# The last chunks routed one by one, and smaller bursts of loads: a DeltaNet block with a routed mixture of experts on one core

## The chip, the cores and the metric

The kernel runs on one core of a Trainium2 chip. The metric is the device time of one execution in microseconds (us). Engines: TensorE multiplies matrices (PE in the profile, PEld for its loads of weights), VectorE (DVE), ScalarE (ACT) and GpSimd (POOL) work elementwise, SyncE (SP) issues most transfers.

## The reference

The first half is DeltaNet attention: 4 batches of 8 heads, 768 tokens of width 48, one state of 48x48 for each batch and head, updated token by token. The second half reads its output as 3072 rows of width 384 and sends each row to one of 16 experts (the best of 4 groups, and in it the best of 4 experts), weighted by both softmaxes.

```python
for t in range(S):
    y[:, :, t] = einsum('bhd,bhde->bhe', q[:, :, t], state)
    v_old = einsum('bhde,bhd->bhe', state, k_n[:, :, t])
    state = state + b_t * einsum('bhd,bhe->bhde', k_n[:, :, t], v[:, :, t] - v_old)
...
ye = maximum(x[rows_of_e] @ w1[g, e], 0) @ w2[g, e]
out[rows_of_e] = g_w * e_w * ye
```

## The kernel before

**Attention.** The 768 tokens are cut into 24 chunks of 32; with 4 batches a chunk has 128 rows, one for each partition. Inside a chunk the token-by-token updates are a triangular system: `gram` (L248) multiplies a chunk's keys and queries with its keys, `inverse(g)` (on VectorE, for four chunks at once) inverts the triangles, and `spread` scales the inverse into the blocks `mtb` that PE takes as weights. `advance(u)` is the recurrence of chunk u. On PE it issues, in this order, a_ps (L486, the state times the keys), o_ps (L495, the state times the queries), w_ps (L503, the inverse times what is left of the values), s_ps (L514, the update of the state, kept in PSUM), and the second part of o_ps (L528). ScalarE copies the results out: f, w, s_bd (the state in SBUF, L520), x (the chunk's output rows). The next chunk's a_ps needs s_bd, so this is a chain from chunk to chunk. Between these matmuls stand a transposition of x (t_ps, L554) and the 20 scores of the gate (l_ps, L451 and L456), and the gram of the chunk ten places ahead (`LEAD`).

**Prologue.** Grams 0 to 9 run ahead of chunk 0. SP loads keys and queries (`load_kq`), the values and keys in another layout (`load_kv`, `kv` in the rows) and constants (`load_con`). All loads after the first go in bursts: `begin` (L797) writes one column of the target from ScalarE, and SP's load waits for that write. The table `bursts` says behind which gram a burst starts; `after_gram` does the same for grams 8 and 9. Two matmuls with 384 columns of constants (L834, 4 in the trace, where each 4-byte matmul is two) stand ahead of chunk 0. Gram 10 is issued in chunk 0, between w_ps and s_ps.

**Routing.** `route(r)` sends a group of chunks, given by `cuts`, to the experts: on VectorE the best score, the one-hot `hots` of the expert and the running count `acc`, on PE the rank of each row in its expert (L451, `s_ps<-hots,con` and `s_ps<-acc,con`), then on VectorE and ScalarE weights, place, the matrices `mine` (what to store) and `at` (where). The sort on PE (L722, `mine` and `at`) adds them into one bank, which holds for each expert's slots the token's row and its weight. The groups are chunks 0-5, 6-11, 12-17, 18-19, 20-21 and 22-23. Sorts of the first chunks are done as they come; in chunk 22 all that are left of chunks 0 to 19 are done, `read_found` (L868) copies the bank to `found`, and `gather_first` starts two indirect gathers of the rows of expert 0 that are known by then from the output x in DRAM. The rows that chunks 20 to 23 add to expert 0 come by matmuls with `at` (`add_near`), and the gathered rows by matmuls with the identity (`add_gathered`, both L852), all into three banks x_ps, which ScalarE copies to `xt_first`.

**Experts.** `order_experts` ranks the experts by their counts; expert 0 is fixed as the first (`FIXED`), the others come in the order of their counts, each with a fixed number of slots. For each expert PE multiplies 48 h_ps matmuls (L1112) and 48 y_ps (L1131); rows come by indirect gathers on POOL and are transposed on PE (t_ps, L1076) for expert 1 first.

**What sets the order.** The whole first half stands under a manual schedule: each engine runs its instructions in the order in which the program issues them. Tasks (`inverse`, `route`) are generators; `work(n)` gives each task a budget in proportion to n and its rate and pushes the ones that have some, and a task that yields a word (`ACT_STEP`, `SORT`, `READY`) is held until `allow` of that word. The main loop for chunk u (L887 to L995) and a tail behind it (L996 to L1030) call them by hand.

## Time and profile before

| | |
|---|---|
| runs of the kernel before | 491.49, 494.62 and 495.47 us, median 494.62 |
| the profiled execution | 493.09 us |
| its span | 491.1 us, mean granted clock of PE 0.976 |
| PE busy | 450.0 us (92% of the span) |
| DVE, ACT, POOL busy | 240.6, 192.8, 176.8 us |
| chunk 1's first a_ps | starts at 46.70 us |
| chunk 23's first a_ps | starts at 206.70 us |
| expert 0's first h_ps | starts at 220.38 us |

A row of the timeline gives the start in us, the busy time, the engine, the line of the kernel, the operation, the tile written and the tiles read, the shape and how many instructions are put together (each matmul of 4-byte data counts twice). In square brackets is the engine's idle time before it and what ended it; "issue" means that nothing which the profile shows ended it. A row of the stretches gives its bounds, its length, the busy time of PE, PEld, DVE, ACT and POOL, the granted clock of PE as a share of full speed, the share of the DMA engines and the rate.

### The profile page before, as it was taken

Reading aid. Unit: us, or ns where it says so; the run is one execution under the profiler, and the core shown is the slowest. Engines: PE = TensorE matmul, PEld = TensorE weight load, DVE = VectorE, ACT = ScalarE, POOL = GpSimd, SP = SyncE. Lnnn points to the kernel's source line nnn. Section 1 sums busy time; section 2 is a strip of 40 time slices with the busy share of each in tenths; the row PEclk is TensorE's granted clock in tenths of the full one; section 3 lists DMA queues with packets and bytes.
Section 4 is the critical chain, followed back from the end, with each engine's and each line's share of the span. In section 5 each row is a group of like instructions: output and inputs, shape, how many; then the busy total and the mean of one; then the engine's idle time right before and its main releaser. Section 6 shows DMA issues by size and latency. Waiting matters only on the chain.

```text
span 491.1 us, 18102 instructions
## 1 busy us (share of the span) xinstructions
PE 450.0 (92%) x7730; PEld 425.9 (87%) x7730; DVE 240.6 (49%) x872; ACT 192.8 (39%) x413; POOL 176.8 (36%) x300
## 2 busy tenths in 40 slices
PE   3338999999999999999999999999999999999992
PEld 3335888888888888789999999999999999999992
DVE  4988998997999998565201201220122112201110
ACT  3335579688897976541112111111211111111120
POOL 0031310415416400103456355544745456255131
PEclk9999599899999999999999999999999999999997
DMA  5566344455434455307977877858997789778820
GB/s 163 149 186 200 100 150 153 128 151 174 144 109 123 145 161 166 90 23 177 370 238 229 277 254 208 300 186 274 318 298 228 255 302 322 248 215 273 308 80 27
DMA packets 56757, 97.07 MB, mean 198 GB/s; under 512 B 18974, under 2 KB 41433, under 8 KB 56675
## 3 DMA queue, kind: packets, MB, share of 16 engines
q1 hardware_dynamic: 50755, 85.89, 54.6%
q0 software_dynamic: 5920, 10.00, 6.5%
q8 instruction: 62, 1.02, 0.9%
q14 instruction: 20, 0.16, 0.1%
HBM read 81.75 MB, written 14.27 MB: 196 GB/s over the span
## 4 chain that ended last, share of the span: by engine, by line
PE 55%; DMA 12%; issue 11%; ACT 7%; DVE 7%; POOL 7%; SPq 0%; POOLq 0%; DVEq 0%
PE y_ps L1131 16%; PE h_ps L1112 16%; DMA out_dram<-yo,to_i 7%; POOL xq L1084 5%; DMA kqt<-in_kq_dram 4%; PE w_ps L503 4%; PE s_ps L514 3%; ACT s_bd L520 3%; PE a_ps L486 2%; PE o_ps L528 2%; PE o_ps L495 2%; DVE m L388 2%; DVE below L382 2%; PE t_ps L554 2%; PE l_ps L456 1%
## 5 line engine op out<-in xcount | busy, mean ns | idle before, releaser
L1131 PE MATMUL y_ps<-hid,w 128*128 128x224 f32 (+15 forms) x768 | 132.2, 332 | 0.0
L1131 PEld LDWEIGHTS y_ps<-hid,w 128*128 128x128 f32 x768 | 129.1, 190 | 0.3
L1112 PE MATMUL h_ps<-xt,w 128*128 128x232 f32 (+14 forms) x720 | 122.7, 330 | 0.0
L1112 PEld LDWEIGHTS h_ps<-xt,w 128*128 128x128 f32 x720 | 120.1, 190 | 0.3
L1084 POOL DMA_INDIRECT xq<-x_dram,from_q x92 | 87.6, 952 | 35.0 <-issue 24.1
L1134 DVE COPY yt<-y_ps 128x232 f32<-128x232 f32 (+13 forms) x14 | 5.1, 365 | 144.4 <-PE y_ps L1131 144.4
L1115 ACT ACTIVATE hid<-h_ps 128x448 f32<-128x448 f32 (+15 forms) x64 | 32.1, 501 | 100.2 <-PE h_ps L1112 98.2
L1143 POOL DMA_INDIRECT out_dram<-yo,to_i x32 | 34.1, 1065 | 93.2 <-DVE yo L1181 83.7
L1136 ACT ACTIVATE yt<-y_ps 128x224 f32<-128x224 f32 (+15 forms) x34 | 11.4, 336 | 116.6 <-PE y_ps L1131 116.6
L382 DVE TENSOR_TENSOR below<-m 128x16 f32<-128x16 f32 (+4 forms) x180 | 53.3, 299 | 0.2
L388 DVE TENSOR_TENSOR m<-m,below 128x16 f32<-128x16 f32 (+4 forms) x180 | 53.0, 295 | 0.4
L520 ACT ACTIVATE s_bd<-s_ps 48x768 f32<-48x768 f32 x46 | 37.0, 804 | 5.6 <-PE s_ps L514 5.1
L1181 DVE TENSOR_SCALAR yo<-yr,gate 128x384 f32<-128x384 f32 (+14 forms) x28 | 11.1, 420 | 39.8 <-DMA yr<-y_dram 31.4
L503 PEld LDWEIGHTS w_ps<-f,mtb 64*64 64x64 f32 x736 | 24.6, 141 | 6.0 <-ACT f L490 3.9
L503 PE MATMUL w_ps<-f,mtb 64*64 64x48 f32 x736 | 27.5, 227 | 1.4 <-ACT f L490 1.4
L427 ACT ACTIVATE mtb<-mt,con 128x256 f32<-128x256 f32 x39 | 28.0, 741 | 0.0
L514 PE MATMUL s_ps<-w,kv 32*112 32x96 f32 x736 | 25.3, 273 | 0.9 <-ACT found L871 0.3
L514 PEld LDWEIGHTS s_ps<-w,kv 32*112 32x112 f32 x736 | 21.3, 178 | 3.8 <-ACT w L507 1.5
L528 PE MATMUL o_ps<-w,gqm 64*64 64x48 f32 x576 | 21.4, 225 | 2.5 <-issue 2.3
L486 PE MATMUL a_ps<-s_bd,kqt 112*32 112x96 f32 x736 | 21.1, 257 | 1.1 <-ACT s_bd L520 1.1
L495 PE MATMUL o_ps<-s_bd,kqt 112*32 112x96 f32 x736 | 21.8, 259 | 0.2 <-issue 0.2
L528 PEld LDWEIGHTS o_ps<-w,gqm 64*64 64x64 f32 x576 | 19.1, 139 | 3.3 <-issue 2.5
(184 smaller groups left out, 543.8 us busy)
## 6 DMA issues: line engine op xcount, KB each, us to landing
w<-in_w_dram SPq DMA_DIRECT2D x29, 1536.0 KB, 10.7
kv<-in_kv_dram SPq DMA_DIRECT2D x24, 416.0 KB, 3.2
kqt<-in_kq_dram SPq DMA_DIRECT2D x20, 448.0 KB, 4.8
x_dram<-x SPq DMA_DIRECT2D x24, 192.0 KB, 2.2
w<-in_w_dram SPq DMA_DIRECT2D x24, 128.0 KB, 3.8
y_dram<-yq SPq DMA_DIRECT2D x36, 84.0 KB, 9.4
yr<-y_dram SPq DMA_DIRECT2D x14, 192.0 KB, 2.5
kqt<-in_kq_dram SPq DMA_DIRECT2D x8, 224.0 KB, 3.6
```

Of the source, the lines that this page charges most:

```text
L382: nc.vector.tensor_tensor(t, column.to_broadcast(like), row.to_broadcast(like), op=ALU.mult)
L388: nc.vector.tensor_tensor(to, to, t, op=ALU.add)
L495: nc.tensor.matmul(o_ps[quads[b], 2 * j:2 * j + 2, :], lhsT=kqt[0:KR, 1, j, quads[b]], rhs=s_bd[0:KR, b, j], start=(j == 0), stop=False, s ...
L503: nc.tensor.matmul(w_ps[b, h], lhsT=mt[b, uu * H + (h % 2) * NP + h // 2], rhs=f[b, h], start=(h == 0), stop=True, skip_group_check=True)
L514: nc.tensor.matmul(s_at[0:KR, b, j], lhsT=k[quads[b], j, 0:KR], rhs=w[quads[b], 2 * j:2 * j + 2], start=(u == 0 and j == 0), stop=True, sk ...
L520: nc.scalar.activation(s_bd[rows, :, :, hh, :], s_at[rows, :, :, hh * D:(hh + 1) * D], ACT.Copy)
L528: nc.tensor.matmul(o_ps[b, h], lhsT=gq[b, hq].rearrange("p a t -> p (a t)"), rhs=w[b, h], start=(u == 0 and h == 0), stop=True, skip_group ...
L1084: nc.gpsimd.indirect_dma_start(out=xq[:, g, :], out_offset=None, in_=x_dram[:, :].rearrange("n (q c) -> (n q) c", q=4), in_offset=bass.Ind ...
L1112: nc.tensor.matmul(h_ps[:, k], lhsT=w1[:, j, (f + k) * 128:(f + k + 1) * 128], rhs=xt[:, j, 0:R], start=(j == 0), stop=(j == DC - 1), skip ...
L1115: nc.scalar.activation(hid[:, f:f + 2], h_ps, ACT.Relu)
L1131: nc.tensor.matmul(y_ps, lhsT=w2[:, f, j * 128:(j + 1) * 128], rhs=hid[:, f], start=(f == 0), stop=(f == FC - 1))
L1143: put = nc.gpsimd.indirect_dma_start(out=out[:, :], out_offset=bass.IndirectOffsetOnAxis(ap=to[0:P, i:i + 1], axis=0), in_=yo[0:P, :], in_ ...
```

## The change

Five things, by the program's own names.

1. **Groups.** `cuts` becomes 0, 6, 12, 18, 20, 21, so chunk 20 is a group of its own, and its rows are sorted ahead of the read of `found`; three chunks (21, 22, 23) instead of four are left for `add_near`. Each of them is routed by a new task, `route_near(u)`, alone. It has its exponential on ScalarE ahead of the ranks, the sums of the weights on POOL, and ranks in a bank of PSUM of its own.
2. **Gathered rows.** `turn_gathered` transposes the gathered rows of expert 0 in six steps into a bank that the scores use otherwise, and one ScalarE copy takes them out as `turned_rows`. VectorE then adds them to the three banks x_ps (`first_in`), where ScalarE copied before.
3. **Order of experts.** `order_experts` runs as a whole behind the addition of `found`, where a first part ran ahead of it.
4. **Prologue.** The bursts are smaller and begin behind earlier grams; chunks 10 and 11 are loaded ahead of chunks 8 and 9, which come last, and chunk 12 is loaded at the end of chunk 0. Gram 10 runs in the prologue, behind gram 9.
5. **spread.** The first block of chunks 16 to 19 is scaled on VectorE instead of ScalarE.

```diff
-            1: [of_kq(RG), of_kq(RG + 1)],
-            RG: [of_kq(RG + 2), of_kq(RG + 3)],
-            RG + 2: [of_kq(u, 1) for u in range(RG)]
-                    + [(wr[:, 0], [lambda: nc.sync.dma_start(out=wr, in_=wr_d)])],
-            2 * RG: [(kv_[0], [lambda: load_kv(0), lambda: load_con(1), lambda: load_kv(1)])],
-            2 * RG + 2: [of_kq(2 * RG), of_kq(2 * RG + 1)],
+            1: [of_kq(u) for u in range(RG, 2 * RG - 1)],
+            RG: [of_kq(2 * RG - 1), of_kq(0, 1), of_kq(1, 1)],
+            RG + 1: [of_kq(2, 1), of_kq(3, 1),
+                     (wr[:, 0], [lambda: nc.sync.dma_start(out=wr, in_=wr_d)])],
+            RG + 2: [(kv_[0], [lambda: load_kv(0), lambda: load_con(1)])],
+            RG + 3: [(kv_[1], [lambda: load_kv(1)]), of_kq(2 * RG + 2)],
+            2 * RG: [(kv_[2], [lambda: load_kv(2)])],
+            2 * RG + 1: [of_kq(2 * RG + 3)],
+            2 * RG + 2: [of_kq(2 * RG)],
+            2 * RG + 3: [of_kq(2 * RG + 1)],
         }
-        after_gram = {2 * RG: [of_kq(2 * RG + 2), (kv_[2], [lambda: load_kv(2)])],
-                      2 * RG + 1: [of_kq(2 * RG + 3), of_kq(NB)]}
...
-            if g in (0, SMALL):
+            vector_first = g in (0, SMALL - 1, SMALL)
+            if vector_first:
                 spread(0, 0, True)
...
-        near = range(NCH - RG, NCH)
-        cuts = [0, 6, 12, 18, near[0], near[2], NCH]
+        near = range(NCH - 3, NCH)
+        cuts = [0, 6, 12, 18, near[0] - 1, near[0]]
...
+        def route_near(u):
...
+            nc.vector.tensor_reduce(best, lg, axis=AX.X, op=ALU.max)
+            nc.vector.tensor_tensor(sx, lg, best[:, :, None].to_broadcast(like), op=ALU.subtract)
+            nc.scalar.activation(ex, sx, ACT.Exp)
...
+            nc.gpsimd.tensor_tensor(ex[:, :, 0:2], ex[:, :, 0:2], ex[:, :, 2:4], op=ALU.add)
...
+            yield RANKS
...
+            in_quarters(r_ps, before, hotf, u == near[0], False)
+            in_quarters(ranks[:, 0:1 + last_one], ones, acc[:, u:u + 1 + last_one], False, True)
...
+            nc.vector.tensor_tensor(rk, r_ps, hotf, op=ALU.mult)
+            nc.vector.tensor_reduce(place[:, u:u + 1], rk, axis=AX.X, op=ALU.add)
...
+            nc.vector.tensor_scalar(at.rearrange("p t i -> p (t i)"), cut["places"],
+                                    place[:, u:u + 1], None, op0=ALU.is_equal)
+            yield WEIGHTS
...
-            for u in range(2 * RG, LEAD):
+            for u in range(2 * RG, LEAD + 1):
                 gram(u, homes[u % len(homes)])
-                begin(after_gram[u])
...
+            def turn_gathered(xg):
+
+                turned_ps = ps.tile([128, DC, 256], F32, tag="g", name="turned_ps")
+                for j in range(DC):
+                    for t, P in enumerate(tiles_of[0]):
+                        nc.tensor.transpose(
+                            out=turned_ps[:, j, t * TILE:t * TILE + P],
+                            in_=xg[0:P, t, j * 128:(j + 1) * 128], identity=ident[0:P, 0:P])
+                nc.scalar.activation(turned_rows, turned_ps[:, :, 0:SLOTS[0]], ACT.Copy)
+
+            def begin_route(u):
+
+                r = {sum(groups[r]): r for r in range(BIG, len(groups))}.get(u)
+                if r is None and u - 1 not in near:
+                    return
+                task = route_near(u - 1) if r is None else route(r)
+                start(task, 1)
+                while held.get(task) is not RANKS:
+                    push(task)
...
+                if NCH - 3 <= u < NCH - 1:
+                    allow(RANKS)
+                    allow(ACT_STEP)
...
-                    while SORT in held.values():
-                        allow(SORT)
+                    while len(sorts) < near[0]:
+                        work(2)
+                        for task in [t for t in behind if held.get(t) is SORT][:1]:
+                            push(task)
...
+                if u == NCH:
+                    add_near(near[:1], range(1, DC))
+                    turn_gathered(gathered)
...
-                nc.scalar.activation(xt_first[:, j], x_in[0][:, j, 0:SLOTS[0]], ACT.Copy)
+                nc.vector.tensor_tensor(xt_first[:, j], x_in[0][:, j, 0:SLOTS[0]],
+                                        turned_rows[:, j], op=ALU.add)
...
-            ordering = order_experts()
-            next(ordering)
...
-            run(ordering)
+            run(order_experts())
```

How the order moves, first on PE at the end of the prologue and in chunk 0 (the lines of the changed kernel are a few higher; `begin_` and `g_ps_` are grams, `s_ps<-con` the two matmuls with constants). Before:

```order
L273 MATMUL begin_104<-kqt_113 32x64 x32
L273 MATMUL g_ps_734<-kqt_114 32x64 x32
L834 MATMUL s_ps<-con 128x384 x2
L503 MATMUL w_ps_855<-vh_688,mtb_827 64x48 x16
L273 MATMUL g_ps_876<-kqt_115 32x64 x32
L514 MATMUL s_ps<-w_872,kv_117 112x96 x16
L528 MATMUL o_ps_693<-w_872,gqm_830 64x48 x16
L486 MATMUL a_ps_874<-s_bd,kqt_106 32x96 x16
```

And in the changed kernel:

```order
L276 MATMUL begin_104<-kqt_113 32x64 x32
L276 MATMUL g_ps_737<-kqt_114 32x64 x32
L276 MATMUL begin_103<-kqt_115 32x64 x32
L854 MATMUL s_ps<-con 128x384 x2
L507 MATMUL w_ps_890<-vh_695,mtb_861 64x48 x16
L518 MATMUL s_ps<-w_907,kv_117 112x96 x16
L532 MATMUL o_ps_700<-w_907,gqm_864 64x48 x16
L490 MATMUL a_ps_909<-s_bd,kqt_106 32x96 x16
```

Gram 10 (`kqt_115`) has moved from between w_ps and s_ps of chunk 0 to the place behind gram 9.

Then VectorE around the read of `found` in chunk 22. Before, chunk 20 and 21's routing starts behind the number cast for the gather (`from_4999<-found_4997`):

```order
L698 TENSOR_TENSOR mine_4893<-hots,what_4896 128x192
L639 TENSOR_SCALAR at_4909<-con,low_4895 128x128
L639 TENSOR_SCALAR at_4911<-con,low_4895 128x128
L297 TENSOR_TENSOR gqm_4915<-gq_3490,con 128x512
L639 TENSOR_SCALAR at_4981<-con,low_4730 128x128
...
L879 CAST from_4999<-found_4997 128x2
L589 TENSOR_REDUCE best_5054<-lg_all 128x10
```

In the changed kernel:

```order
L633 TENSOR_SCALAR at_4833<-con,low_4817 128x128
L467 TENSOR_TENSOR vh_4835<-kv_119,normt_3772 128x2x4x48
L593 TENSOR_REDUCE best_4896<-lg_all 128x5
...
L612 TENSOR_TENSOR acc<-acc,hots 128x16
L300 TENSOR_TENSOR gqm_4927<-gq_3490,con 128x512
L650 TENSOR_TENSOR rk_4972<-rk_4972,hots 128x16
...
L677 TENSOR_TENSOR mine_4978<-hots,what_4981 128x96
L633 TENSOR_SCALAR at_5000<-con,low_4980 128x128
L633 TENSOR_SCALAR at_5025<-con,low_4743 128x128
...
L899 CAST from_5043<-found_5041 128x2
```

Chunk 20's seven rows from `best` to `acc`, and its fourteen from `rk` to `at`, now stand ahead of the cast.

Last, PE in chunk 22. Before, the ranks of the group 18-19 stand behind chunk 21's o_ps, and the sorts follow w_ps:

```order
L528 MATMUL o_ps_4783<-w_4819,gqm_4607 64x48 x16
L451 MATMUL s_ps<-hots,con 32x32 x4
L451 MATMUL s_ps<-acc,con 32x32 x4
L486 MATMUL a_ps_4827<-s_bd,kqt_115 32x96 x16
L495 MATMUL o_ps_4935<-s_bd,kqt_115 32x96 x16
L554 MATMUL t_ps_4952<-con,x_4877 128x128 x3
L503 MATMUL w_ps_4958<-f_4933,mtb_4450 64x48 x16
L722 MATMUL s_ps<-mine_3745,at_4376 128x96
...
L514 MATMUL s_ps<-w_4975,kv_118 112x96 x16
```

In the changed kernel:

```order
L532 MATMUL o_ps_4784<-w_4854,gqm_4607 64x48 x16
L490 MATMUL a_ps_4862<-s_bd,kqt_115 32x96 x16
L499 MATMUL o_ps_4947<-s_bd,kqt_115 32x96 x16
L455 MATMUL s_ps<-hots,con 32x16 x4
L455 MATMUL s_ps<-acc,con 32x16 x4
L558 MATMUL t_ps_4983<-con,x_4923 128x128 x3
L507 MATMUL w_ps_5002<-f_4945,mtb_4450 64x48 x16
L691 MATMUL s_ps<-mine_3745,at_4523 128x96
...
L691 MATMUL s_ps<-mine_4978,at_5000 128x96
L518 MATMUL s_ps<-w_5019,kv_118 112x96 x16
```

The ranks of chunk 20 stand between chunk 22's o_ps and its w_ps, ahead of which the ranks of 18-19 stood in chunk 21; the sorts are ten in both: the first of before has moved a chunk earlier, and chunk 20's (`mine_4978`) is new.

More of the change, by code (lines that the diff above doesn't have):

```diff
@@ L19 @@
 SHARE = 0.61
-LEAD = 10
+LEAD, IDLE = 10, 2
 FIXED, TILE = 1, 128
@@ L24 @@
 SPREAD = "spread"
+RANKS, WEIGHTS = "ranks", "weights"
 BEGUN, SORT, ROOTS, FACTOR, READY = "roots begun", "sorting", "roots made", "factor made", "inverse ready"
@@ L438, in inverse @@
             yield READY if g else ACT_STEP
-            if g:
+            if not vector_first:
                 spread(0, 0)
@@ L639, in turn_to @@
                 (nc.gpsimd if early else nc.vector).tensor_scalar(
-                    at[:, 0] if one else at.rearrange("p t i -> p (t i)"),
-                    cut["places"][:, 0:TILE] if one else cut["places"],
-                    low[:, u - u0:u - u0 + 1] if one else place[:, u:u + 1], None,
+                    at[:, 0], cut["places"][:, 0:TILE], low[:, u - u0:u - u0 + 1], None,
                     op0=ALU.is_equal)
@@ L677, in route @@
                 yield
[L678 to L688 removed]
+            nc.vector.tensor_reduce(place[:, u0:u0 + n], rk, axis=AX.X, op=ALU.add)
@@ L689, in route @@
+            yield
+            at_u = place[:, u0:u0 + n]
+            nc.vector.tensor_scalar(half[:, :, 0], at_u, float(TILE), None, op0=ALU.is_lt)
+            nc.vector.tensor_scalar(half[:, :, 1], at_u, float(TILE), None, op0=ALU.is_ge)
+            yield
+            nc.vector.scalar_tensor_tensor(low, in0=half[:, :, 1], scalar=-float(TILE),
+                                           in1=at_u, op0=ALU.mult, op1=ALU.add)
+            yield
             nc.vector.reciprocal(what[:, u0:u0 + n, 2:3], cw)
@@ L690, in route @@
             yield
[L691 to L706 removed]
+            to_both, like = [128, n, T, 3], [128, n, T * 3, NE]
@@ L707, in route @@
+            (nc.gpsimd if early else nc.vector).tensor_tensor(
+                what2, what[:, u0:u0 + n, None, :].to_broadcast(to_both),
+                half[:, :, :, None].to_broadcast(to_both), op=ALU.mult)
+            (nc.gpsimd if early else nc.vector).tensor_tensor(
+                mine, hotf[:, :, None, :].to_broadcast(like),
+                what2.rearrange("p n t c -> p n (t c)")[:, :, :, None].to_broadcast(like),
+                op=ALU.mult)
             if early:
                 yield SOON
-            elif not final and not one:
-                for u in us:
-                    turn_to(u)
@@ L712, in route @@
             for g, u in enumerate(us):
-                if one:
-                    for v in us[:2] if u == u0 else us[g + 1:g + 2]:
-                        turn_to(v)
+                for v in us[:2] if u == u0 else us[g + 1:g + 2]:
+                    turn_to(v)
                 at = ats[u]
@@ L846, in deltanet_then_moe @@
             allow(FACTOR)
-            ahead_of = {u: [u + LEAD] if u + LEAD < NCH else [] for u in range(NCH + 1)}
+            ahead_of = {u: [u + LEAD] if u and u + LEAD < NCH else [] for u in range(NCH + 1)}
             begun, x_in = set(), {}
@@ L946, in deltanet_then_moe @@
                     gram(v)
-                if ahead_of[u] or later or ending:
+                if ahead_of[u] or not u or later or ending:
                     next(step)
@@ L973, in deltanet_then_moe @@
                 allow(ROOTS)
-                for r in range(EARLY, len(groups)):
-                    if u == sum(groups[r]) + (r < BIG):
-                        start(route(r), 0.4 if r < BIG else 0.6 if r == BIG else 1)
+                for r in range(EARLY, BIG):
+                    if u == sum(groups[r]) + 1:
+                        start(route(r), 0.4)
                 allow(SOON)
```

175 lines of the change are left out of this document (75 added, 100 removed).

## The prediction

> **What bounds the kernel now.** I read the page's slices first, then the stretches around the places that the change touches, then the rows of the timeline there. From the page, busy tenths and granted clock in slices of 12.3 us, and the queue that brings instructions:
>
> ```profile
> PE   3338999999999999999999999999999999999992
> DVE  4988998997999998565201201220122112201110
> PEclk9999599899999999999999999999999999999997
> q8 instruction: 62, 1.02, 0.9%
> ```
>
> PE is full from slice 4 (about 40 us) to the end, so after the prologue time is won only by letting PE start earlier, by taking work or idle time from it, or by giving it a faster clock. VectorE (DVE) is as full until slice 16, some 200 us, and idles later. One slice, the fifth, has a clock of 0.5. The stretches (from:to length, busy of PE, PEld, DVE, ACT, POOL, clock, DMA share, GB/s):
>
> ```profile
> 8.00:10.00 2.00, 0.00 (x0) 0.00 (x0) 1.31 (x2) 0.59 (x2) 0.42 (x3) 1.00 0.83 227
> 41.00:44.00 3.00, 2.87 (x128) 2.50 (x126) 2.55 (x18) 2.51 (x5) 0.02 (x1) 1.00 1.02 280
> 44.40:47.80 3.40, 1.58 (x65) 1.52 (x69) 3.40 (x20) 1.43 (x3) 0.00 (x0) 1.00 0.39 121
> 47.80:61.40 13.60, 13.60 (x270) 11.82 (x260) 13.53 (x54) 8.48 (x18) 4.43 (x15) 0.50 0.33 104
> 61.40:75.00 13.60, 13.26 (x460) 11.84 (x458) 13.26 (x54) 11.09 (x23) 1.33 (x6) 1.00 0.48 154
> 190.00:200.00 10.00, 9.40 (x316) 7.94 (x312) 8.49 (x40) 6.52 (x16) 0.00 (x0) 1.00 0.44 127
> ```
>
> So PE runs at half rate from 47.8 to 61.4 us, though busy all the time, right behind a stretch in which it was busy 1.58 of 3.40 us. The change touches two places: the start, to chunk 1's first a_ps, and the ending, from chunk 20 to the first h_ps.
>
> The start (start, us, engine, line; in brackets the idle time before and what ended it):
>
> ```profile
> 11.22 2.30 PE L273 MATMUL begin<-kqt 48*32 48x64 f32 x128 [3.62 <-DMA kqt<-in_kq_dram]
> 28.29 0.56 DVE L463 TENSOR_TENSOR vh<-kv,normt 128x384 f32<-128x384 f32 x1 [1.43 <-DMA kv<-in_kv_dram]
> 34.64 1.17 PE L273 MATMUL begin<-kqt 48*32 48x64 f32 x64 [6.21 <-DMA kqt<-in_kq_dram]
> 36.83 2.93 PE L834 MATMUL s_ps<-con 128*128 128x384 f32 x4
> 39.69 1.71 PE L503 MATMUL w_ps<-vh,mtb 64*64 64x48 f32 x32
> 41.33 0.86 PE L273 MATMUL g_ps<-kqt 48*32 48x64 f32 x64
> 42.12 1.04 PE L514 MATMUL s_ps<-w,kv 32*112 32x96 f32 x32
> 42.40 0.60 ACT L278 ACTIVATE gt<-g_ps 128x256 f32<-128x256 f32 x1
> 42.79 0.43 ACT L284 ACTIVATE gq<-g_ps 128x256 f32<-128x256 f32 x1
> 43.22 1.62 ACT L520 ACTIVATE s_bd<-s_ps 48x768 f32<-48x768 f32 x2
> 43.09 0.79 PE L528 MATMUL o_ps<-w,gqm 64*64 64x48 f32 x20
> 46.22 0.55 PE L528 MATMUL o_ps<-w,gqm 64*64 64x48 f32 x12 [2.35 <-issue]
> 46.70 0.87 PE L486 MATMUL a_ps<-s_bd,kqt 112*32 112x96 f32 x32
> ```
>
> The chain: chunk 8's keys land at 34.6 us, grams 8 and 9, the dummies of L834, w_ps, gram 10, s_ps, o_ps, a_ps(1). The 2.35 us lie inside one row of 32 equal matmuls (20 before, 12 after), so no operand and no semaphore can be their cause. I take them for a wait for instructions: 62 packets hold 1.02 MB, 16 KB each, and until 44 us the loads fill the DMA engines (share 1.02).
>
> The ending:
>
> ```profile
> 192.01 0.26 DVE L662 TENSOR_TENSOR rk<-rk,hots 128x96 f32<-128x96 f32 x1 [0.60 <-ACT rk L627]
> 195.33 0.19 DVE L589 TENSOR_REDUCE best<-lg_all 128x10 f32<-128x40 f32 x1
> 197.01 0.68 DVE L297 TENSOR_TENSOR gqm<-gq,con 128x512 f32<-128x512 f32 x1
> 198.17 0.19 DVE L662 TENSOR_TENSOR rk<-rk,hots 128x32 f32<-128x32 f32 x1
> 200.62 0.68 DVE L297 TENSOR_TENSOR gqm<-gq,con 128x512 f32<-128x512 f32 x1
> 201.61 0.96 DVE L639 TENSOR_SCALAR at<-con,low 128x128 f32<-128x128 f32 x4 [0.31 <-PE s_ps L722]
> 203.92 1.04 PE L514 MATMUL s_ps<-w,kv 32*112 32x96 f32 x32 [0.34 <-ACT found L871]
> 206.89 0.20 DVE L589 TENSOR_REDUCE best<-lg_all 128x10 f32<-128x40 f32 x1 [2.82 <-ACT lg_all L566]
> 220.38 9.24 PE L1112 MATMUL h_ps<-xt_first,w 128*128 128x224 f32 x48
> 225.52 0.97 POOL L1067 DMA_INDIRECT xg<-x_dram,from_i  x1 [18.68 <-DVE picked L1043]
> 233.38 0.49 PE L1076 MATMUL t_ps<-con,xg 128*128 128x128 f32 x3
> ```
>
> DVE makes the `at` of the last sorts until 202.57; the sorts end, `found` is read, and chunk 22's s_ps follows at 203.92, waiting for that read. From there to the first h_ps are 16.46 us. After it PE is fed to the end.
>
> **The change part by part.** All against the profiled execution, 493.09 us (span 491.1 and 1.99 outside it), 1.5 under the median 494.62.
>
> *The loads.* kv0 goes in a burst of its own earlier, so the 1.43 us before vh go from the DVE chain. From the second gram on, whose burst moves at 8:10, I count 6.3 MB of loads up to chunk 9's keys; at 280 GB/s (41:44) that is 22.5 us, at 227 (8:10) 27.8. From some 8.5 us on, chunk 9 lands between 31 and 36; I take 33, and chunk 8 ahead of it. Then come gram 9 and gram 10 (1.17 each, by gram 8's row), the evacuation of gram 10, whose bank the dummies need (0.60 + 0.43), and the dummies (2.93): 33 + 1.17 + 1.17 + 1.03 + 2.93 = 39.3 for w_ps(0), before 39.69; ends 38.4, where DVE's inverse would hold it, and 40.5, short of the slowest landing. Gram 10 has gone from between w_ps and s_ps: its 0.86 covered the evacuation of w, which is now bare, an estimated 0.65 (w_ps ends at 41.40, s_ps starts at 42.12). ACT's two evacuations of gram 10, which held s_bd until 43.22, lie earlier. Then 39.3 + 1.71 (w_ps) + 0.65 (evacuation of w) + 1.04 (s_ps, of which s_bd's first half needs a part) + 1.62 (s_bd) and 0.2 to start: a_ps(1) at 44.5, ends 43.5 and 45.6. Before it was at 46.70. So **−2.2** (−1.1 to −3.2), if the 2.35 us do not come again. Why they should not: the block of instructions that was missing at 43.9 is asked for a fixed number of PE instructions earlier; with gram 10 moved ahead, PE passes that point some 5 to 7 us earlier, before a stretch of 6 us in which it waits for chunk 8 in any case, and the wait for it lies under that one.
>
> *The half rate.* These are the a_ps of chunks 2, 3 and 4; chunk 1's started at 46.70:
>
> ```profile
> 57.28 1.51 PE L486 MATMUL a_ps<-s_bd,kqt 112*32 112x96 f32 x32
> 65.96 0.87 PE L486 MATMUL a_ps<-s_bd,kqt 112*32 112x96 f32 x32
> 73.06 0.87 PE L486 MATMUL a_ps<-s_bd,kqt 112*32 112x96 f32 x32
> ```
>
> Periods of 10.58, 8.69 and 7.10 us; the first two exceed the third by 3.48 + 1.59 = 5.1. The clock fell behind a stretch with PE busy 1.58 of 3.40; a second drop stands behind 2.40 of 3.41, and the stretch 61.4:75 kept its clock with 13.26 of 13.60:
>
> ```profile
> 85.36:88.77 3.41, 2.40 (x60) 2.20 (x60) 3.41 (x12) 2.12 (x5) 1.62 (x7) 1.00 0.44 133
> 88.77:92.18 3.41, 3.41 (x71) 2.80 (x63) 3.41 (x11) 1.78 (x5) 2.62 (x10) 0.50 0.33 79
> ```
>
> Without the stall chunk 0 has two short gaps left (the evacuation of w, s_bd), 0.65 each and close together: some 2.1 of 3.4 us busy in the worst place, between the 1.58 that cost the clock and the fullness that kept it, and below the 2.40 that cost it for one window. So the drop may come in a shorter form; I put it at gone in somewhat over half the cases. Ends: 0 and **−5.1**; I take −5.1, since the only drop of this length follows the only stall of this length. DVE can follow: it is ahead of PE by its waits for kv and POOL between 82 and 115 us.
>
> The Trainium skill, in "TensorE: Matmul & The Clock Gate", section "Part 1: The HAM clock gate", has the clock halved only after an idle window of about 3.4 us, and whole again after one such window of work. By that the 2.35 us would cost nothing but themselves, the half rate would have a cause that the change does not touch, and the sum would be 5.1 higher; the trace differs in both points (1.58 us of work in the stretch ahead, and 13.6 us of full work before the clock came back), so I go by the trace and keep the rule's case as the second rival.
>
> *spread.* One spread of chunk 16's group goes from ACT to DVE: 0.47 us more on DVE, and PE's f(16) some 0.6 earlier, which ends at the ending's wait for DVE and is worth nothing there.
>
> *The ending.* Chunk 20 is now routed alone ahead of `found`. Its first part is the seven rows from 195.33 to 197.01, 1.68 us; its second, from 198.17 to 200.62, 2.45, less the second `at` of 128x128 (0.24) and some width, 2.05. Together 3.7 us more on DVE ahead of the last `at` rows, less the 0.60 and 0.31 that it idles there: 2.8; with the spread's 0.47, s_ps(22) comes 3.3 later. PE meets new waits for DVE, too: the ranks of both small groups now stand ahead of w_ps(21) and w_ps(22), so what queues behind them is the recurrence itself. From s_ps(22) to h_ps I walk the changed order with the old durations: ranks of chunk 21 among the matmuls of chunk 23 (+0.33), its exponential ahead of the evacuation of x(23) (+0.2), against a last routing for one chunk instead of two, weights on POOL beside it, six transposes in the place of twelve rows into x_ps, and no three ACT copies ahead of h_ps: 15.9 instead of 16.46. So the ending is 3.3 − 0.55 = **+2.75**. Bounds: 0 − 0.55 if DVE's chain is not late (it idles 2.82 us before 206.89, so it gains back what comes after), and 3.7 + 0.47 − 0.55 = 3.6 if none of the idle time is usable.
>
> *Ordering of experts.* `order` now runs after the last sums; its result, and so expert 1's row list, comes 3 to 4.6 us later against h_ps. The gather issued at 225.52 is needed by t_ps at 233.38, 7.9 us later, and its landing takes 4.1 (median of two, the issues of DMA from 224 to 232 us):
>
> ```profile
> xg<-x_dram,from_i POOLq DMA_INDIRECT x2, 4.1
> ```
>
> The 3.8 us of cover are about used up. I take nothing; with the cover gone it costs up to 1 us.
>
> The sum: 493.09 − 2.2 − 5.1 + 2.75 = **488.5 us**.
>
> **The rivals.**
> *The half rate comes anyway* (the two short gaps set it off, or it hangs on something else): −2.2 + 2.75 on 493.09 is 493.6. For it: the drop behind 2.40 of 3.41. Against it: that one lasted one window.
> *DVE is not late at the ending*: since all of chunk 20 stands so much earlier in DVE's list, its idle time elsewhere may swallow it; 493.09 − 7.3 − 0.55 = 485.2. Against: DVE has 1.5 us idle of 10 in 190:200, not 3.7.
> *Instructions still wait behind the loads*, the side on which it gets slower. The loads now come without pauses, and every block of instructions has to pass them. Where the DMA engines were full, the block, asked for one block's length of matmuls before the hole, at about 40.8, was there at 46.22: 5.4 us. With 16 KB for some 127 loads of weights and their matmuls (62 packets for the program), five blocks lie from gram 4 to o_ps(0). Taken one after the other from gram 4 (11.22) they end at 38, at gram 10's end; with 1.03 and 2.93 behind it w_ps(0) comes at 42.0, and a_ps(1), 5.2 later as above, at 47.2 instead of 46.70. It decides if PE has less than 5.4 us between two blocks of waiting that is there anyway; then nothing is won, the half rate stays, and the ending's loss alone is left: 493.09 + 0.5 + 2.75 = 496.3. For it: the stall itself; against it: PE has 6.2 us to spare before 34.64.
>
> The Trainium skill, in "DMA: Bandwidth & Descriptors", section "Queues, rings and completion order", says that each DMA engine takes turns between its queues by packets. By that a block would wait for one packet per engine and not for a whole load, and this rival would fall away; the 2.35 us at a share of 1.02 rather bear it out, and no row shows the block itself.
>
> *The change does less than it says*: chunk 9 lands no earlier than 36. Then the start wins nothing but the stall, 490 to 495 with the half rate gone or not; it has no chance of its own and lies between the first two.
>
> **How the numbers follow.** The forecast has 0.45, the half rate that stays 0.28, DVE in time 0.10, instructions behind loads 0.17. Over 1%, about what a measurement of this kernel can tell from no change, is below 489.7 or above 499.6 against the median: nearly all of the forecast (its own range, from both ends of the start and of the ending, is 486 to 491) and of DVE in time lie below, with a little of the second case at a shorter half rate: 0.45 faster. The second case and the rival on the slow side lie within, but for an ending at its worst with a late expert 1: 0.06 slower, 0.49 the same. The range is 485 to 496.5, from DVE in time to the slow side.
>
> **What would show it.** A row of o_ps(0) unbroken, a_ps(1) at 44 to 45.5 us, and no stretch of clock 0.5 after it: the start is right. A hole marked "issue" inside a row of matmuls between 30 and 50, with a 0.5 behind it, makes it wrong. At the ending, chunk 22's s_ps should start some 3 us later after chunk 21's a_ps than now, with PE's idle time ahead of ranks, w_ps or `found` put down to DVE; if that distance is unchanged the +2.75 is wrong. The distance from s_ps(22) to h_ps should be 15 to 17 us, and t_ps of expert 1 should wait for its gather less than 1 us.

## The result

The changed kernel takes 498.34 us (median of 6, 495.86 to 501.48) against 494.38 us (median of 6, 491.49 to 495.47): a ratio of 1.0109, 95% interval 1.0073 to 1.0144. It is slower by about 1%, where 488.5 was forecast. In a second series of runs the ratio was 1.0153 (1.0081 to 1.0226). Here and below a median is over all runs, while a ratio with its interval leaves out the slow ones (well above the kernel's fastest, at a lower granted clock), so a ratio need not be the quotient of two medians. The profiled execution is the shortest of the six, 495.86 us with a span of 494.1.

From the page of the changed kernel, the rows that answer to those of before:

```profile
PE   3438999999999997889999999999999999999992
DVE  4997999999999999265101210220122012210110
PEclk9999999999999999899999999999999999999997
q8 instruction: 62, 1.02, 0.9%
```

The 0.5 in the fifth slice is gone, as forecast. In its place PE has a dent in slices 16 to 18 (185 to 222 us), with a small one in the clock: the ending. The stretches show both:

```profile
44.40:47.80 3.40, 2.73 (x98) 2.46 (x99) 3.40 (x21) 3.33 (x6) 0.00 (x0) 1.00 0.56 166
47.80:61.40 13.60, 13.06 (x445) 11.35 (x447) 13.53 (x55) 12.12 (x25) 4.04 (x13) 1.00 0.50 154
191.90:195.30 3.40, 1.89 (x76) 1.55 (x72) 3.09 (x19) 1.71 (x4) 0.00 (x0) 1.00 0.36 71
202.10:205.50 3.40, 2.54 (x84) 2.11 (x80) 0.36 (x2) 1.79 (x3) 1.89 (x2) 1.00 0.35 94
205.50:208.90 3.40, 3.40 (x71) 2.79 (x64) 0.89 (x5) 1.22 (x4) 1.44 (x7) 0.50 0.21 75
```

The start, from the timeline of the changed kernel:

```profile
27.43 1.32 PE L276 MATMUL begin<-kqt 48*32 48x32 f32 x101 [3.62 <-issue]
33.30 1.17 PE L276 MATMUL begin<-kqt 48*32 48x64 f32 x64 [4.55 <-DMA kqt<-in_kq_dram]
34.76 1.14 PE L276 MATMUL g_ps<-kqt 48*32 48x64 f32 x62 [0.28 <-DMA kqt<-in_kq_dram]
36.92 0.88 PE L276 MATMUL begin<-kqt 48*32 48x64 f32 x38 [0.60 <-issue]
38.71 2.93 PE L854 MATMUL s_ps<-con 128*128 128x384 f32 x4 [0.91 <-ACT gq L287]
41.57 1.17 PE L507 MATMUL w_ps<-vh,mtb 64*64 64x48 f32 x32
43.33 1.04 PE L518 MATMUL s_ps<-w,kv 32*112 32x96 f32 x32 [0.59 <-ACT w L511]
44.30 1.14 PE L532 MATMUL o_ps<-w,gqm 64*64 64x48 f32 x32
46.11 0.87 PE L490 MATMUL a_ps<-s_bd,kqt 112*32 112x96 f32 x32 [0.68 <-ACT s_bd L524]
```

Chunk 9's keys land at 34.76, not at 33; gram 10 has a hole of its own; the dummies wait 0.91 for its evacuation. o_ps(0) is unbroken, but w_ps starts at 41.57 against 39.69, and a_ps(1) at 46.11 against 46.70: 0.6 us won instead of 2.2. Chunk 4's a_ps comes at 67.94 against 73.06, so the half rate that is missing brings the rest, 4.5 us.

The first row is a wait marked "issue" inside a run of equal matmuls, like the hole of 2.35 us in chunk 0. In the kernel before it is 1.24 us long:

```profile
27.10 1.33 PE L273 MATMUL begin<-kqt 48*32 48x32 f32 x101 [1.24 <-issue]
28.08 0.29 ACT L800 ACTIVATE kqt<-con 128x1 f32<-128x1 f32 x2
```

The second row here is ScalarE's write that starts the loads of chunks 8 and 9. It stands on ScalarE behind the evacuation of the gram in which the hole is, and in all thirteen profiles it starts 0.98 us behind the hole's end: in the changed kernel at 28.41. The smaller bursts bring the grams ahead of it earlier, but the longer hole takes that back, and chunk 8's load starts 0.3 us later than before.

And the ending:

```profile
196.04 0.26 PE L455 MATMUL s_ps<-hots,con 128*32 128x16 f32 x8 [1.89 <-DVE hots L610]
199.09 1.97 PE L691 MATMUL s_ps<-mine,at 128*128 128x96 f32 x14 [0.35 <-DVE at L633]
201.41 1.04 PE L518 MATMUL s_ps<-w,kv 32*112 32x96 f32 x32 [0.34 <-ACT found L891]
212.63 0.55 PE L558 MATMUL t_ps<-con,x 128*128 128x128 f32 x3 [0.76 <-DVE hot L715]
220.70 1.59 PE L1144 MATMUL h_ps<-xt_first,w 128*128 128x224 f32 x7 [1.09 <-DVE found L1054]
```

PE waits 1.89 us for chunk 20's one-hot matrix ahead of its ranks, 0.76 for the output of chunk 23, and 1.09 for VectorE's additions ahead of h_ps. From chunk 21's a_ps to chunk 22's s_ps are 15.71 us (12.64 before), from there to h_ps 19.29 (16.46). At h_ps the changed kernel is 0.3 us behind (220.70 against 220.38), and from there to the end it takes 273.4 us against 270.7; the timeline shows three short holes there (0.40, 0.72 and 0.19 us) that the profile of before does not have, 1.3 of the 2.7.

### The profile page after: what moved, and what is told of

Same layout as the page of the kernel before. It is cut to its first block, busy times and chain, and to the rows that moved or that the text cites. A ratio compares the mean times of both kernels' runs of the same rounds, so it can differ in the third digit from the quotient of the medians.

```text
span 494.1 us, 18159 instructions
## 1 busy us (share of the span) xinstructions
PE 447.3 (91%) x7736; PEld 419.8 (85%) x7736; DVE 243.7 (49%) x895; ACT 191.8 (39%) x411; POOL 181.8 (37%) x321
## 4 chain that ended last, share of the span: by engine, by line
PE 37%; DVE 32%; issue 11%; DMA 10%; POOL 6%; ACT 1%; another core or an unknown queue 1%; POOLq 0%; SPq 0%; DVEq 0%
PE h_ps L1144 15%; PE y_ps L1163 15%; DVE m L391 9%; DMA out_dram<-yo,to_i 7%; DVE below L385 6%; POOL xq L1116 5%; DMA kqt<-in_kq_dram 3%; DVE corner L385 2%; DVE vh L467 2%; DVE gqm L300 2%; PE begin L276 1%; POOL out_dram L1175 1%; DVE mt L419 1%; DVE m L316 1%
## 5 line engine op out<-in xcount | busy, mean ns | idle before, releaser
L507 PEld LDWEIGHTS w_ps<-f,mtb 64*64 64x64 f32 x736 | 23.6, 135 | 5.4 <-ACT f L494 2.9
L518 PE MATMUL s_ps<-w,kv 32*112 32x96 f32 x736 | 24.3, 267 | 1.5 <-ACT w L511 0.6
L276 PE MATMUL begin<-kqt 48*32 48x64 f32 (+1 forms) x576 | 9.9, 280 | 16.1 <-issue 6.7
L321 POOL MEMSET m<- 128x256 f32 (+4 forms) x30 | 4.2, 192 | 52.3 <-DVE m L316 52.3
L276 PEld LDWEIGHTS begin<-kqt 48*32 48x32 f32 x576 | 8.2, 144 | 17.3 <-issue 12.6
```

What stands on the lines that cost most here:

```text
L276: nc.tensor.matmul(g_out[quads[b], hh * NP + j, of], lhsT=kqt[rows, 0, j, quads[b]], rhs=kqt[rows, of, j, quads[b]], start=True, stop=True ...
L507: nc.tensor.matmul(w_ps[b, h], lhsT=mt[b, uu * H + (h % 2) * NP + h // 2], rhs=f[b, h], start=(h == 0), stop=True, skip_group_check=True)
L518: nc.tensor.matmul(s_at[0:KR, b, j], lhsT=k[quads[b], j, 0:KR], rhs=w[quads[b], 2 * j:2 * j + 2], start=(u == 0 and j == 0), stop=True, sk ...
```

## The experiments

Every run shows four distances that carry the comparison: the start of chunk 1's a_ps (a1), chunk 21's a_ps to chunk 22's s_ps (A), from there to the first h_ps (B), and from h_ps to the end (C). The last column is the granted clock's drops to 0.5 up to 470 us, as start and length.

| profiled execution | us | a1 | A | B | C | drops |
|---|---|---|---|---|---|---|
| before | 493.09 | 46.70 | 12.64 | 16.46 | 270.7 | 47.8: 13.65; 88.8: 3.41 |
| before, again | 488.62 | 44.23 | 12.03 | 19.18 | 271.5 | 200.4: 3.41 |
| loads_only | 489.17 | 44.32 | 11.96 | 19.08 | 271.1 | 157.0: 3.41; 201.4: 3.41 |
| prologue_only | 495.97 | 48.52 | 11.96 | 17.55 | 272.9 | 69.0: 6.83; 123.6: 3.41 |
| ending_only | 495.49 | 45.38 | 15.99 | 17.97 | 273.6 | 45.5: 3.41 |
| changed | 495.86 | 46.11 | 15.71 | 19.29 | 273.4 | 205.5: 3.41 |
| changed, again | 500.18 | 47.02 | 16.42 | 20.05 | 272.5 | 91.4: 3.41; 200.6: 13.65 |
| after_gram_back | 496.50 | 44.74 | 17.56 | 19.91 | 271.7 | 197.5: 13.65 |
| four_singly | 500.86 | 48.02 | 17.32 | 21.12 | 270.8 | 159.7: 6.83; 200.6: 13.65 |
| four_behind_found | 494.59 | 45.12 | 12.32 | 21.02 | 272.8 | 65.6: 6.83; 202.2: 3.41 |
| ranks_behind_w | 496.14 | 45.30 | 16.25 | 20.44 | 271.4 | 88.9: 3.41; 198.2: 13.65 |
| old_tail | 499.02 | 46.87 | 16.90 | 19.57 | 271.9 | 103.8: 6.83; 199.4: 13.65 |
| filled_gap | 502.31 | 44.70 | 15.34 | 19.34 | 274.1 | 88.1: 3.41; 112.0: 3.41; 173.4: 6.83; 211.0: 3.41 |

The totals of one kernel spread widely (the kernel before from 486.23 to 502.98 in 20 runs of one job), so verdicts on totals go by medians and intervals, and the steps are read from the distances.

**The two halves.** The first takes the new prologue alone, the second the rest of the change without the prologue (the edits of the diff above, each applied without the other).

```diff
 # prologue_only, on the kernel before: the new bursts, and
-            for u in range(2 * RG, LEAD):
+            for u in range(2 * RG, LEAD + 1):
```

> The kernel before with only the new prologue (smaller bursts, chunks 8 and 9 loaded last, gram 10 behind gram 9, chunk 12 loaded at the end of chunk 0). Theory: the start wins what the two profiles show up to chunk 3's a_ps, 5.7 us, and keeps it to the end: 488 to 490 us, with chunk 23's a_ps near 201 and expert 0's first h_ps near 214.7. Rival: what the start wins is given back behind it, since VectorE's list of work sets the time of chunk 20 and the expert stage was 2.7 us longer in the changed kernel: 491 to 494.

> The changed kernel with the old prologue (old bursts, gram 10 in chunk 0). Theory: the whole loss lies in the ending, 3.1 us up to chunk 22's s_ps and 2.8 from there to the first h_ps: 499 to 502 us, with the distance from chunk 21's a_ps to chunk 22's s_ps near 15.7 and from there to h_ps 18 to 20. Rival: VectorE has time in hand when the start is late, so that chunk 20's routing is hidden here: 494 to 497.

Measured: prologue_only 492.74 us (median of 9) against 491.64 (median of 20) for the kernel before, ratio 1.0075 (1.0026 to 1.0125); ending_only 498.84, ratio 1.0225 (1.0147 to 1.0303). The theory of a start that wins falls: against the kernel before, over many runs, the new prologue loses a little. The ending loses in full: A is 15.99, as expected, and B at 17.97 and the total are just under the ranges given. The prologue alone shows where its loss sits:

```profile
36.94 1.13 PE L275 MATMUL g_ps<-kqt 48*32 48x64 f32 x61 [2.20 <-DMA kqt<-in_kq_dram]
40.34 2.93 PE L835 MATMUL s_ps<-con 128*128 128x384 f32 x4 [0.90 <-ACT gq L286]
45.73 1.04 PE L516 MATMUL s_ps<-w,kv 32*112 32x96 f32 x32 [0.59 <-ACT w L509]
48.52 0.87 PE L488 MATMUL a_ps<-s_bd,kqt 112*32 112x96 f32 x32 [0.68 <-ACT s_bd L522]
```

Chunk 9's keys came at 36.94 here, and gram 10, the wait for its evacuation and the bare evacuation of w follow one another.

**The loads without gram 10.**

```diff
 # on the kernel before: the new bursts, chunk 12 at the end of chunk 0, and
             for u in range(2 * RG, LEAD):
                 gram(u, homes[u % len(homes)])
-                begin(after_gram[u])
```

> The kernel before with the new bursts of loads, but gram 10 in its old place between chunk 0's w_ps and s_ps. Theory: moving gram 10 is what took the wait marked issue out of chunk 0, so here a hole of 1.5 to 3 us stands in chunk 0 and the half rate follows it: 492 to 495 us. Rival: the loads alone do it, because no load is left to collide with at 41 to 46 us: no hole of over 1 us in chunk 0, no clock of 0.5 before 85 us, 488 to 490.

Measured: 490.20 us (median of 12), ratio 1.0025 (0.998 to 1.0071), no difference. The rival's picture holds: no hole in chunk 0 and a_ps(1) at 44.32.

```profile
34.80 1.17 PE L275 MATMUL g_ps<-kqt 48*32 48x64 f32 x64 [1.44 <-DMA kqt<-in_kq_dram]
35.90 2.93 PE L835 MATMUL s_ps<-con 128*128 128x384 f32 x4
38.75 1.95 PE L505 MATMUL w_ps<-vh,mtb 64*64 64x48 f32 x32
40.63 0.98 PE L275 MATMUL g_ps<-kqt 48*32 48x64 f32 x64
42.51 1.13 PE L530 MATMUL o_ps<-w,gqm 64*64 64x48 f32 x32
44.32 0.87 PE L488 MATMUL a_ps<-s_bd,kqt 112*32 112x96 f32 x32 [0.68 <-ACT s_bd L522]
```

So moving gram 10 is not what takes the hole away. What it costs is read best from the start of gram 9, since chunk 9's keys land anywhere from 34.76 to 38.20 us with the same new loads: from there to a_ps(1) are 11.35 to 11.86 us in the four profiles with gram 10 in the prologue and 8.67 to 9.52 in the six with it in chunk 0, so it costs 1.8 to 3.2 us. Nor are the waits marked "issue" gone: the one at about 27 us, which holds up the loads of chunks 8 and 9, is 3.62 to 6.36 us long in the ten profiles with the new loads, against 1.15 to 2.06 in the three with the old ones. But the total of loads_only, too, is that of the kernel before, which raised the question whether the hole belongs to that kernel at all.

**The two kernels again.**

> The kernel before, unchanged, profiled a second time. Theory: the hole of 2.35 us in chunk 0 and the 13.65 us at half rate behind it are an accident of that one execution, and this one shows its sparse stretches and its drops of the clock at other places or for another length, with a total up to 5 us away from 493.09. Rival: hole and half rate belong to the kernel and stand again at 43 to 62 us, with chunk 3's a_ps near 66.

> The changed kernel, unchanged, beside the next two on one chip. Theory: 1 to 2% slower than the kernel before (five to nine us), with 15.5 to 16 us from chunk 21's a_ps to chunk 22's s_ps again (12.64 in the kernel before), and drops of the clock at other places than in its first profile. Rival: the distance is an accident as well, and lies within 1 us of 12.64.

Measured: 488.62 us in that one execution. Chunk 0 and the stretch that ran at half rate in the first profile of the kernel before:

```profile
41.93 0.79 PE L528 MATMUL o_ps<-w,gqm 64*64 64x48 f32 x20
43.75 0.55 PE L528 MATMUL o_ps<-w,gqm 64*64 64x48 f32 x12 [1.03 <-issue]
44.23 0.87 PE L486 MATMUL a_ps<-s_bd,kqt 112*32 112x96 f32 x32
...
47.80:61.40 13.60, 12.98 (x442) 11.18 (x430) 13.50 (x53) 11.02 (x23) 5.59 (x19) 1.00 0.49 161
```

The hole stands between the same two matmuls, 20 before and 12 after, but is 1.03 us long instead of 2.35; a_ps(1) is at 44.23, and the clock stays whole. ending_only, which has the old loads too, has the hole at the same place, 2.27 us long, with a drop of 3.41 us. So the place of the hole belongs to the old loads (all three profiles with them have it, none of the ten with the new ones), and its length and what the clock does differ from execution to execution: 13.65 us, none and 3.41. The changed kernel again: 500.85 us (median of 6), with A at 16.42; this A is no accident.

**Chunk 20's routing.** Four runs ask what in the ending costs. Base is the changed kernel (four_singly) or the changed kernel with gram 10 back in chunk 0 (the others).

```diff
 # four_singly: near is chunks 20 to 23, route_near for each, begun in the chunk behind it
-        near = range(NCH - 3, NCH)
+        near = range(NCH - 4, NCH)
...
 # after_gram_back
-            for u in range(2 * RG, LEAD + 1):
+            for u in range(2 * RG, LEAD):
...
 # four_behind_found: as four_singly with gram 10 back, but chunk 20 begun with chunk 21,
 # behind the read of found
+                    tasks = [route_near(v) for v in {near[2]: near[:2]}.get(u, [u - 1] if u > near[2] else [])]
...
 # ranks_behind_w: chunk 20's ranks behind chunk 22's w_ps
-                if NCH - 3 <= u < NCH - 1:
+                if u == NCH - 3:
                     allow(RANKS)
                     allow(ACT_STEP)
...
+                if ending:
+                    allow(RANKS)
+                    allow(ACT_STEP)
```

> The changed kernel with chunk 20 left out of the sorts ahead of found and routed singly behind it like 21 to 23 (four single routings, groups end with 18 to 19). Theory: VectorE's 3.7 us ahead of found are what PE waits for; s_ps of chunk 22 comes 2.5 to 3.5 us earlier, no clock of 0.5 between 200 and 212, and the total is 489 to 492 us. Rival: the loss lies in the single routings and in the additions on VectorE ahead of h_ps, and a fourth one adds to it: 495 to 498.

> The changed kernel with gram 10 back between chunk 0's w_ps and s_ps, all else as changed. Theory: gram 10 ahead of chunk 0 costs a matmul burst, a bare evacuation and, most times, a wait for instructions: chunk 1's a_ps comes at 44 to 45 us instead of 46 to 48, and the total is 2 to 4 us under that of the changed kernel in the same job. Rival: the gain at chunk 1 is taken up by VectorE's list at chunks 20 to 22, and the total is the same within 1 us.

> The kernel of the run before this one, but chunk 20 is routed singly behind the read of found, together with chunk 21, instead of alone ahead of it. Theory: VectorE's list ahead of found is as short as in the kernel before, so chunk 22's s_ps comes 11.5 to 13 us after chunk 21's a_ps instead of 15.7, with no idle time of PE over 0.5 us ahead of chunk 22's w_ps; the total is 2.5 to 5 us under that run. Rival: the routing of chunk 20 delays the ending wherever it stands, and what is won ahead of s_ps stands between s_ps and h_ps (over 19 us): the total is the same within 1 us.

> The same base, with chunk 20's ranks moved behind chunk 22's w_ps on PE and their evacuation behind that of w on ScalarE. Theory: the sorts and the read of found wait for VectorE's list, not for PE, so PE's idle time moves behind w_ps and chunk 22's s_ps still comes 15 to 17 us after chunk 21's a_ps. Rival: the ranks ahead of w_ps hold up the recurrence, and without them s_ps comes 1.5 to 2 us earlier (13.5 to 14.3).

four_singly was a miss: 509.30 us (median of 6, 499.55 to 509.83). Its chunk 20 is begun ahead of found all the same, and its exponential stands on ScalarE ahead of x(21) and f(22). VectorE reaches it late, ScalarE stands still, and PE with it; right behind that the clock falls:

```profile
199.19 0.87 PE L499 MATMUL o_ps<-s_bd,kqt 112*32 112x96 f32 x32 [2.34 <-ACT x L541]
...
196.20:199.20 3.00, 0.66 (x34) 0.44 (x26) 2.69 (x16) 0.66 (x3) 0.28 (x2) 1.00 0.00 0
200.70:214.20 13.50, 13.16 (x205) 12.25 (x201) 2.55 (x12) 5.08 (x11) 3.83 (x11) 0.50 0.25 72
```

after_gram_back: 496.11 us (median of 12), ratio 1.0087 (1.0048 to 1.0125), with a1 at 44.74; the changed kernel in the same job had 1.0153, so gram 10's place is worth about 3 us, though the two intervals overlap. four_behind_found: A falls to 12.32, with nothing over 0.36 us ahead of w_ps, as the theory had it. But B grows to 21.02 and the total, 495.85 us (median of 12), ratio 1.0076 (1.0036 to 1.0116), is that of the run before it: here the rival is right. What a shorter A wins, chunk 20's rows in x_ps, its ranks and the other waits take back in B. ranks_behind_w: 497.35 us (median of 6), ratio 1.0122 (1.0056 to 1.0188); A is 16.25; the idle time goes behind w_ps and VectorE's list still holds up the sorts:

```profile
195.87 0.26 PE L455 MATMUL s_ps<-hots,con 128*32 128x16 f32 x8 [0.37 <-DVE hots L610]
196.59 0.88 PE L691 MATMUL s_ps<-mine,at 128*128 128x96 f32 x6 [0.40 <-ACT sx L625]
198.92 3.30 PE L691 MATMUL s_ps<-mine,at 128*128 128x96 f32 x14 [1.45 <-DVE at L633]
```

The last 14 sorts run at half rate here, 3.30 us against 1.97 in the changed kernel. Without that A would be about 14.9, against 15.3 to 16.0 where the clock stayed whole: less than the rival's 1.5 to 2 us, but the place of the ranks may count for some tenths up to 1 us.

**The clock in the ending.** The gap ahead of chunk 20's ranks filled with work that nobody reads, on the base with gram 10 back. They start new sums in the bank of the sorts, and what the earlier chunks had put there is taken to be lost, so this kernel leaves out those rows' places and its output is of no use; its other instructions and their order are the same.

```diff
+                if u == NCH - 2:
+                    for _ in range(9):
+                        nc.tensor.matmul(s_ps[:, 0, 480:512], lhsT=ident,
+                                         rhs=con[:, cols[1]:cols[1] + 32],
+                                         start=True, stop=True, skip_group_check=True)
```

> The changed kernel with gram 10 back in chunk 0 (the earlier run of that edit had PE idle 1.91 us ahead of chunk 20's ranks and a half rate of 13.65 us behind it), and nine matmuls of 32 columns with the identity, whose result nobody reads, ahead of those ranks. Theory: PE's idle time sets off the drop of the clock, so with the gap filled no drop begins between 194 and 200 us, chunk 22's s_ps still comes 15 to 16.5 us after chunk 21's a_ps, and the total is 1 to 5 us lower than the run without them. Rival: the drop has another cause and comes as often, or the fillers delay the ranks: no drop missing, total the same or up to 2 us higher.

Measured: 493.56 us (median of 13), ratio 1.0058 (1.0021 to 1.0096), against 1.0087 without the filling, an interval that overlaps it; the total alone decides nothing. The same place in the two kernels, first after_gram_back:

```profile
193.00:197.50 4.50, 2.59 (x102) 2.18 (x91) 4.09 (x22) 1.47 (x5) 0.00 (x0) 1.00 0.46 133
197.60:211.10 13.50, 13.16 (x191) 11.81 (x189) 3.72 (x21) 4.25 (x10) 3.56 (x9) 0.50 0.14 43
```

then filled_gap (this execution as a whole is 9 us over its kernel's median, with three drops earlier on):

```profile
198.00:202.00 4.00, 4.00 (x99) 3.77 (x99) 3.66 (x18) 1.03 (x3) 0.00 (x0) 1.00 0.53 145
202.00:208.00 6.00, 5.36 (x93) 4.63 (x87) 2.96 (x19) 2.02 (x6) 0.51 (x1) 1.00 0.02 4
```

The clock stays whole through the sorts; A is 15.34, so VectorE's list still sets it (the last sorts wait 0.30 us for its `at`). Over all profiles: of the seven with idle PE time of 1.4 to 2.4 us at this place, five show a drop of 13.65 us right behind it or, in ranks_behind_w, from its middle on; of the six without, none does.

Every run, not the profiled one alone, has its mean granted clock on record, and it bears this out. In filled_gap seven of 13 runs have 0.993 or more, in after_gram_back none of 12. The kernel before was run three times beside the others; the median clock of the seven sets of runs without the gap lies between 0.984 and 0.993, that of six of the seven sets with it between 0.970 and 0.983. The exception is the first six runs of the changed kernel, with 0.992.

The profiles also show when the gap is paid for. The drops of one execution begin and end on one grid of 3.41 us: in filled_gap they begin at 88.1, 112.0, 173.4 and 211.0, apart by 7, 18 and 11 times 3.41. The grid lies differently in each execution. In the five profiles with the long drop one stretch of the grid held most of the gap, or a part of it and other holes, and PE was busy 1.43 to 1.95 us of its 3.41. In ending_only a boundary at 195.64 cuts the gap (194.91 to 196.82) in two, with 2.32 and 2.24 us busy on its sides, and the clock stays whole; in the first profile of the changed kernel, cut at 195.28, the sides have 1.93 and 2.65.

**The tail.**

```diff
-                    turn_gathered(gathered)
+                    add_gathered(gathered, [0, 1])
...
-                nc.vector.tensor_tensor(xt_first[:, j], x_in[0][:, j, 0:SLOTS[0]],
-                                        turned_rows[:, j], op=ALU.add)
+                nc.scalar.activation(xt_first[:, j], x_in[0][:, j, 0:SLOTS[0]], ACT.Copy)
```

> The same base, with the gathered rows added by matmuls into x_ps as in the kernel before and copied by ScalarE, in the place of transposes, a copy and additions on VectorE. Theory: the additions that stand bare between the last x_ps and the first h_ps, 1.09 us of idle PE in every run of the changed kernel so far, shrink to under 0.5, PE has 0.5 to 0.8 us more work in x_ps, and s_ps of chunk 22 to the first h_ps is shorter by 0 to 0.7 us. Rival: ScalarE's copies stand as bare as VectorE's additions, and the idle time stays at 1 us or more.

Measured: 499.23 us (median of 6), ratio 1.0184 (1.0133 to 1.0235), its a1 at 46.87. The wait ahead of h_ps falls as expected, B by 0.34 to 19.57; the total is no better for it, and why this kernel's runs are the longer ones stays open; in the profiled one a late start (chunk 9's keys at 38.20 against 35.85 on its base) is part of it.

```profile
225.28 0.99 PE L1139 MATMUL h_ps<-xt_first,w 128*128 128x224 f32 x4 [0.43 <-ACT xt_first L1039]
```

## Why the prediction was wrong, by its own steps

From the profile that the sum starts from to that of the changed kernel, the time grew by 2.8 us, where 4.6 less was forecast. Of this miss of 7.4 us the start makes 1.6, the half rate 0.6, the stretch from s_ps(22) to h_ps 3.4 and the expert stage 2.7; the rest came out 0.9 better. But that profile is no typical execution of the kernel before: it has a long drop in chunk 0 and none in the ending, so the steps are judged against the others too.

1. **The half rate, −5.1: the step that failed.** The forecast saw that the drop followed the hole, and that the hole would go; both came true in the changed profile, which wins 4.5 us by it. But it took one execution for the kernel. The kernel before in its second profile has the same hole at 1.03 us and no half rate, and reaches 488.62, which is the forecast itself without any change. Over 60 runs its mean granted clock is 0.985, which loses some 7.4 us of 491; the last 6.4 us of the span (in both profiles), which run at 0.5 with PE done, are 3.2 of these. So all other drops together lose an estimated 4 us in a mean execution, half of the 8.5 in the first profile, and a credit of 5.1 for one of them was not there to be had. The changed kernel pays drops of its own, by the same estimate 3 us in its first six runs (mean clock 0.989) and 6 in the second six (0.984). The rival "the half rate comes anyway" named a condition, not this.

2. **The loads and gram 10, −2.2.** The sum was made against 46.70, an a_ps(1) that held the 2.35 us. Against 44.23 the changed prologue comes 1.9 to 2.8 us later (46.11, 47.02), not 2.2 earlier: chunk 9 lands at 34.76 instead of 33, gram 10 has a hole (0.60), and the dummies wait for its evacuation (0.91). That gram 10's new place takes the hole out was wrong: loads_only has none with gram 10 in its old place; and gram 10's evacuation of 1.03, costed at 39.3 in the sum, was paid for nothing. The sum held that a wait for instructions would lie under the wait for chunk 8 in any case. It stands ahead of it instead: the 3.62 us at 27.43 hold back the write that starts chunk 8's load. The rival on the slow side had the sign and nearly the size of this step (a_ps(1) at 47.2), and part of its mechanism: no row shows what a wait marked "issue" waited for, but with the new loads those ahead of chunk 8 grew, as it said. It had w_ps(0) at 42.0, where 41.57 and 41.70 were measured. Its total of 496.3, close to 495.86, is luck: it kept the half rate in chunk 0, which went, and had 2.75 for the ending, which took 5.9 more, and nothing for the expert stage.

3. **VectorE ahead of found, +3.3: right.** A grew from 11.96 to 12.64 (kernels with the old ending) to 15.71 (3.1 to 3.8 us), and four_behind_found, where it is 12.32 again, shows that it is VectorE's list that sets it. The ranks as what the recurrence waits for were named; their place on PE matters little (ranks_behind_w).

4. **From s_ps(22) to h_ps, −0.55: wrong sign.** Without a drop in that stretch it is 16.46 and 17.55 with the old ending and 17.97 with the new one: +0.4 to +1.5; with one drop of 3.41 us it is 19.08 and 19.18 with the old and 19.29 and 19.34 with the new one. So most of the 2.8 us between the first two profiles is a drop that the kernel before has in its second profile too. The walk was right that PE gets less to do: it is busy 14.95 us of the stretch in ending_only against 15.92 in the kernel before, both at a whole clock. But what it stands idle grows from 0.54 to 3.02, of which three waits of the new ending are 2.1: 0.28 at chunk 21's ranks, 0.76 ahead of t_ps of chunk 23 (ScalarE's copy of that chunk's output stands behind the exponential, which waits for VectorE; put at 0.2), and 1.09 for VectorE's additions; old_tail puts the last at 0.66 of its 1.09.

5. **What was not in the sum.** PE's idle time in the ending sets off a drop of the clock there, in five of seven profiles with that gap for 13.65 us. From chunk 21's a_ps to h_ps the two executions with it and the same ending take 36.47 and 37.47 us (after_again, after_gram_back), the one with the gap and no drop (ending_only) 33.96: 2.5 to 3.5 us. The forecast knew the mechanism from chunk 0 and used it only where the change would take it away, not where it would bring it about.

6. **Expert 1's late rows, 0: right.** t_ps of expert 1 runs at 233.80 with no wait. The 2.7 us between h_ps and the end can't be put down to the change: with the same stage ending_only has 273.6, but after_gram_back 271.7 and four_singly 270.8, and the profiles with the old stage have 270.7 to 272.9. Why one execution takes longer there stays open.

From the second profile of the kernel before to the first of the changed one the steps add up: 488.62, +1.9 at a1 (44.23 to 46.11), +3.8 from chunk 21's a_ps to h_ps (31.21 to 35.00, each with one drop of 3.41 us) and +1.9 in C make 496.2, where 495.86 was measured. None of the versions tried beats the kernel before; loads_only can't be told from it.

## What to carry to other kernels

The length of a stall with no releaser, and the clock stretch behind it, can differ from one execution to the next: profile the kernel before a second time, and look at the mean granted clock of all its runs, ahead of crediting a change with removing it. Such a stall may also move to another place: ask what is started behind it there. Where work is moved onto an engine that is the limit, count not only its time but what PE does in the meantime: an idle gap of about 2 us can cost its own length again in clock, or nothing, by where it falls. And an instruction with a late operand, put ahead of the evacuations on an engine that runs in order, holds up everything behind it, as the exponential of four_singly did.
